# Fourier mixing and a routed expert layer on one core: the order of the second batch's loads and of its first stage at the start of the kernel

## The chip, the cores and the metric

The kernel runs on one core of one Trainium2 chip. The metric is the device time of the program in microseconds (us), median of the runs shown. One more execution was taken with the hardware profiler; every duration below that is not a median comes from that one.

## The reference, cut to what matters

```python
X = np.fft.fft(x, axis=1)              # x: (8, 2496, 256), over the sequence of 2496
x = np.fft.fft(X, axis=2).real         # over the 256 features; then (19968, 256) tokens
logits = x @ w_gate                    # 8 experts
e = argmax(logits); g = softmax(logits)[e]
h = np.maximum(x @ w1[e], 0.0)         # w1[e]: 256 x 1024
out = g * (h @ w2[e])                  # w2[e]: 1024 x 256, rows in the order of the tokens
```

Each of the eight batches is transformed, every token is sent to the one expert with the largest logit, and the expert's two matrix products follow. All data are 32-bit floats.

## The kernel before, in words

**Two parts.** The Fourier part works batch by batch. The sequence length is split as 2496 = 104 x 24. The first stage does the transforms of length 104, the second stage those of length 24, and in the same second stage a matmul (tile p, `p3` in the code) does the 256 features and the gate logits. The expert part works block by block: 128, 256 or 512 rows of one expert, fetched from a table of sorted rows in DRAM, `Xs`. A list made ahead of time (`rounds`, `in_order`) says which blocks may be computed once the rows of which batches are in `Xs`. The blocks of batch 0 alone are two of 256 and four of 128 rows.

**Loads of x.** A batch's x comes in three pieces of 896 KB (q = 0, 1, 2; tile xq, three buffers), each asked for by `load(b, q)` (L285, issue at L294) on the queue of SyncE (SP). Batch 0's third piece is asked for in two halves (L301).

**First stage.** `first(b)` (L387 to L410) is a generator of twelve steps, three for each of four rounds. Rounds 0 to 2 fold piece q on VectorE (`fold`, L320, and `fold_d`, L309 to L311: add and subtract mirrored rows and columns). Rounds 1 to 3 multiply the piece before on TensorE (`half1`, tile s, twice two columns), copy the result on ScalarE (L335, tile t) and write it to a DRAM tensor `Td` (L405; for batch 1 on ScalarE's queue); then `load` asks for the piece of the next batch into the freed buffer. In the text below the steps are counted 1 to 12: step 1 is the first fold of piece 0, steps 4 and 7 the first folds of pieces 1 and 2, steps 5, 8, 11 the first half of the products of pieces 0, 1, 2, and steps 6, 9, 12 the second half with the write to `Td`. Piece 2's second half is longer than the others: ten matmul instructions instead of four. After step 12, `ahead_of` (L991) asks with `regroup` (L414, issue at L417) for two DMAs that read `Td` back in the order that the second stage needs (tile t4s).

**Batch 0's first stage** is `first_whole` (L339). It doesn't go through DRAM: each of its twelve columns is sent by one SBUF-to-SBUF DMA of 110 KB from tile t (t1 in the code, two buffers) to every twelfth partition of t4s (L371), even columns on ScalarE's queue, odd ones on SP's. Loads of batch 1 stand between them on SP's queue: piece 0 ahead of column 9, pieces 1 and 2 behind column 11 (L373 and L374).

**Second stage.** `second(b)` (L425) is a generator of 19 steps, k = 0 to 18. Step 0 reads t4s (tile pr, L435), steps 1 and 2 transform the first two groups, each of steps 3 to 7 and 11 to 15 transforms one group more (tile p2 into zz, L443), multiplies for the features (tile p3) and makes the rows on VectorE (L474, twice); steps 8 to 10 and 16 to 18 are the routing of a half (`route`, L480 to L522: arg max, softmax, position in the expert's list). p3, p2, s and pr share three PSUM buffers. `send` (L526) sends 128 rows to their places in `Xs` with one indirect DMA of GpSimd (L237); a batch has 20 of them.

**The order of the work** is written out by the driver (L1054 to L1093): every engine executes its instructions in the order in which these generators are advanced. Before the change `early = ahead_of(1)`, batch 1's first stage, is advanced three steps ahead of `second(0)`, and then once after each even step k from 4 on, eight times in all. What is left of it, step 12 and the regrouping, comes later in `side`, woven with the making of the block table (`close`, `plan`, L542 on), while `experts` waits for its first table, for the sends and for twelve more steps of `side`.

**At the start** (L1015 to L1038) POOL asks for a table of constants, for `rt` and `wg` (from which a small product, tile pg, makes part of the table), for the constants of the plan (`bt`) and writes a block of padding rows to `Xs`. TensorE multiplies ones, WARM = 60 times, while x is on its way.

Of the kernel before, what the change touches and what calls it, by code (L numbers as in the profile page):

```python
# [12 lines left out]
F32 = mybir.dt.float32  # L13
# [7 lines left out]
B, S, D = 8, 2496, 256  # L21
# [3 lines left out]
NQ = NS // 4  # L25
# [4 lines left out]
NP = 112  # L30
# [6 lines left out]
E, F = 8, 1024  # L37
FC = F // 128
BIG, BLK, REST = 512, 256, 128
CAP = NT + BLK  # L40
# [11 lines left out]
def bc(ap, axis, n):  # L52
    shape = list(ap.shape)
    shape.insert(axis, n)
    return ap[tuple([slice(None)] * axis + [None])].to_broadcast(shape)
# [75 lines left out]
def rounds():  # L131

    want = [((256, 2), (128, 4)), ((256, 4),)] + [((512, B),)] * (B - 2)
    plan, used = [], 0

    def full(done, size):
        return max(0, -(-(done - used - E * (size - 1)) // size))

    for b in range(B):
        done = (b + 1) * S
        now = []
        for size, most in want[b]:
            k = min(full(done, size), most)
            if k:
                now.append((size, k, False))
            used += size * k
        if b == B - 1:
            k = full(done, BLK)  # L150
            used += BLK * k
            now.append((BLK, k, False))
            now.append((REST, (NT - used + E * (REST - 1)) // REST, True))
        plan.append(now)
    return plan
# [29 lines left out]
LATE = 4  # L185
SHARE, EARLY, ROOM = 0.6, 0.7, 1.2
AHEAD = 12
WARM = 60
MOST = max(k for now in rounds() for _, k, _ in now)


def halved(b, size):

    return size == 512 and b > 2 or size == 256 and b == B - 1
# [7 lines left out]
def block_consts():  # L202
    c = {
        "i": np.arange(MOST),
        "e9": np.arange(E + 1),
        "low": (np.arange(E)[None, :] <= np.arange(E)[:, None]).reshape(-1),
        "cap": CAP * np.arange(E),
    }
    at, k = {}, 0
    for n, v in c.items():  # L210
        at[n] = (k, k + len(v))
        k += len(v)
    return np.concatenate(list(c.values())).astype(np.float32)[None], at
# [3 lines left out]
def kernel(ctx: ExitStack, tc, x, w_gate, w1, w2, out):  # L217
    nc = tc.nc
    vec, act, pool = nc.vector, nc.scalar, nc.gpsimd

    def mm(o, lhsT, rhs, start=True, stop=True, **kw):
        nc.tensor.matmul(o, lhsT=lhsT, rhs=rhs, start=start, stop=stop, **kw)  # L222

    Td = [nc.dram_tensor(f"Td{b}", (NP, NS * D), F32, kind="Internal").ap() for b in range(B)]
    Xs = nc.dram_tensor("Xs", (ROWS, W), F32, kind="Internal").ap()

    def const_dram(name, v):
        return nc.inline_tensor(v, name=f"c_{name}").ap()

    def unordered(ins, group):  # L230
        ins = getattr(ins, "ins", ins)
        tc.declare_no_dep(ins, group=group, reason="no row is written twice")
        tc.add_to_no_dep_group(group, ins)
        return ins
# [7 lines left out]
    def sent(ins, b):  # L242
        tc.declare_no_dep(ins, group="taken", reason="no block before this batch's round has these rows")
        tc.add_to_no_dep_group(f"xs{b}", ins)
# [9 lines left out]
    xp = ctx.enter_context(tc.tile_pool(name="xp", bufs=2))  # L254
# [5 lines left out]
    pad = cp.tile([128, W], F32, name="pad")  # L260
# [9 lines left out]
    con, k = {}, 0  # L270
# [9 lines left out]
    wg = cp.tile([128, 2, E], F32, name="wg")  # L280
# [6 lines left out]
    def load(b, q, parts=1):  # L287

        if b < B:
            xq = xp.tile([NP, 8, D], F32, tag="xq", name="xq", bufs=3)  # L290
            row = (b * NQ + q) * NA
            ahead[b, q] = xq[0:NA]
            if parts == 1:
                nc.sync.dma_start(out=xq[:].rearrange("p j d -> p (j d)"), in_=x[row:row + NP])  # L294
                return iter(())
            return pieces(xq, row)

    def pieces(xq, row):

            for k in range(2):  # L300
                nc.sync.dma_start(  # L301
                    out=xq[:].rearrange("p (c j) d -> p c j d", c=2)[:, :, 2 * k:2 * k + 2],
                    in_=x[row:row + NP].rearrange("p (c j d) -> p c j d", c=2, d=D)[:, :, 2 * k:2 * k + 2])
                yield

    def fold_d(o, a, n):

        lo, hi = free(a, 1, [D, n], [1, H - 1]), free(a, D - 1, [D, n], [-1, H - 1])
        vec.tensor_tensor(free(o, 1, [D, n], [1, H - 1]), lo, hi, op=ALU.add)  # L309
        vec.tensor_tensor(free(o, H + 1, [D, n], [1, H - 1]), lo, hi, op=ALU.subtract)  # L310
        vec.tensor_copy(free(o, 0, [D, n], [H, 2]), free(a, 0, [D, n], [H, 2]))  # L311
# [27 lines left out]
    def first_whole():  # L339

        pm0 = xp.tile([NA, D], F32, tag="pm0", name="pm0")
        for q in range(NQ):
            xq = ahead.pop((0, q))
            t1 = xp.tile([NP, 4, D], F32, tag="t1", name="t1")
            for lo in (0, 2):
                end = q == NQ - 1 and lo
                a, m = xq[:, lo:lo + 2], xq[:, 4 + lo:6 + lo]
                n = 2
                if end:
                    n = 1  # L350
                    fold_d(pm0[:], m[:, 1], 1)
                vec.tensor_tensor(a[:, 0:n], a[:, 0:n], m[:, 0:n], op=ALU.add)
                fold_d(m, a, 2)
                ps = pm_.tile([NP, 2, D], F32, tag="m", name="s1")
                for i in range(2):
                    s = 4 * q + lo + i
                    o = ps[0:NR, i]
                    if s < NS - 1:
                        mm(o, columns(s), m[:, i])
                        continue  # L360
                    for k, l, r in ((NS - 1, 0, H + 1), (NS + 1, H + 1, D)):
                        mm(o[:, l:r], columns(k), pm0[:, l:r], True, False)
                        mm(o[:, l:r], columns(k + 1), m[:, 1, l:r], False, True)
                if end:
                    for i in range(2):
                        act.copy(t1[0:NR, lo + i], ps[0:NR, i])
                else:
                    act.copy(t1[0:NR, lo:lo + 2], ps[0:NR])
                for i in range(2):
                    s = 4 * q + lo + i  # L370
                    (nc.sync if s % 2 else act).dma_start(out=t4s[s:GP:NS, 0:NG], in_=t1[0:NR, lo + i])  # L371
            if q:
                load(1, q - 1)  # L373
        load(1, NQ - 1)  # L374
        for lo in range(0, NS + 3, 5):
            natural(lo, lo + 5)
        for h in range(2):
            ahead[0, "t4", h] = t4s[:, h * HALF:(h + 1) * HALF]

    def columns(s):  # L380
        return wp[:, s]

    def natural(lo, hi):
        n = hi - lo
        vec.tensor_copy(free(con["w1"][:, lo:hi], 0, [NP, n], [2 * NU, NG], [1, 2 * NU]),
                 free(wp[:, lo:hi], 0, [NR, n], [1, NG], [NG, 2 * NU]))
# [36 lines left out]
    zz = cp.tile([128, 2, NW * 128], F32, name="zz")  # L423
# [102 lines left out]
    def send():  # L526

        if waiting:
            b, place, idx, rows = waiting.popleft()
            if b:  # L530
                due = sp.tile([128, 1], F32, tag="due", name="due", bufs=8)
                act.copy(due[:], place)  # L532
                pool.tensor_copy(idx, due[:])  # L533
            sent(put_row(Xs, idx, rows, E * CAP - 1, "xs"), b)


    cv, where = block_consts()
    bt = cp.tile([1, cv.shape[1]], F32, name="bt")
# [463 lines left out]
    def mixed(b):  # L1002
# [22 lines left out]
    came = cp.tile([1, 1], F32, name="came")  # L1025
    pool.tensor_copy(came[:], wp[0:1, NS + 2, 0:1])
    pool.dma_start(out=table[:], in_=const_dram("table", packed))
    pool.dma_start(out=con["rt"][:], in_=const_dram("rt", consts["rt"]))
    pool.dma_start(out=wg[:], in_=w_gate)
    pool.dma_start(out=bt[:], in_=const_dram("blocks", cv))  # L1030
    sent(unordered(pool.dma_start(
        out=Xs[E * CAP:].rearrange("(k p) w -> p k w", k=BLK // 128), in_=bc(pad[:], 1, BLK // 128)), "xs"), 0)
    for k in range(WARM):
        pw = pse.tile([128, D], F32, tag="bd"[k % 2], name="py")
        mm(pw[:], ones[:], bc(ones[:], 1, 2))
# [4 lines left out]
    tabs, whole = {}, set()  # L1040
    todo = in_order()
    first_whole()
    vec.tensor_copy(tri[:], con["tri"][:])
    for c in range(2):
# [10 lines left out]
    for _ in range(3):  # L1055
        next(early)
    for k, _ in enumerate(second(0)):
        if k > 3 and k % 2 == 0:
            next(early, None)
        send()  # L1060
    work = experts(todo)
    steps = {b: mixed(b) for b in range(1, B)}
    for b in range(1, B):
# [6 lines left out]
        blocks = [(size, k * size / BIG, halved(b - 1, size)) for size, k, _ in rounds()[b - 1]]  # L1070
        total = sum(k * (15 if seven_ else 16) for _, k, seven_ in blocks)
        open_ = sum(k * (8 if seven_ else 16) for _, k, seven_ in blocks)
        while done < total:
            w, full = next(work)
# [72 lines left out]
```

## Time and profile before

| | |
|---|---|
| median of 3 runs | 1264.88 us (1259.51 to 1265.91) |
| profiled execution | 1264.07 us, span of its trace 1262.3 us |
| TensorE busy | 1213.0 us, 96% of the span |
| VectorE, ScalarE, GpSimd busy | 763.6, 430.8, 449.2 us |
| mean granted TensorE clock | 0.979 |
| TensorE busy in 0 to 110 us, and from there to 1262 us | 73.4 of 110 us; 1139.7 of 1152 us |

The trace counts from the start of the span; 1.8 us of the profiled execution lie outside of it. PE is TensorE's matmul, PEld its weight load, DVE VectorE, ACT ScalarE, POOL GpSimd, SP SyncE; a q behind the name of an engine is its sequencer, which issues DMAs. In a line of the timeline the first number is the start in us, the second the duration, then engine, line of the code, operation, output and input tile, and in brackets how long the engine stood idle before and what it waited for. In a line of the chain of waits stand start, duration, and the work that the end of the program was waiting for at that time.

### The profile page before, as it was taken

What the parts mean: (1) busy time and instruction counts of PE and PEld (TensorE: products, weight loads), DVE (VectorE), ACT (ScalarE), POOL (GpSimd) and SP (SyncE); (2) the same over time, 40 slices, a digit from 0 to 9 for tenths busy, and PEclk for the clock granted to TensorE, in tenths of its full rate; (3) what the DMA queues carried; (4) which work ended last, traced back from release to release, by engine and by line L of the source; (5) the groups of instructions that cost most, each with busy time, mean ns of one, the idle gap of its engine ahead of it and who ended that gap; (6) DMA issues with size and microseconds to landing.
All of it is one profiled execution on the core that took longest, in us unless ns stands there. A gap on an engine that the chain in (4) does not pass through costs nothing.

```text
span 1262.3 us, 22419 instructions
## 1 busy us (share of the span) xinstructions
PE 1213.0 (96%) x7333; PEld 1080.0 (86%) x7333; DVE 763.6 (60%) x1820; ACT 430.8 (34%) x1168; POOL 449.2 (36%) x533
## 2 busy tenths in 40 slices
PE   6759999999999999999999999999999999999997
PEld 3648898777788899888988899889999999999996
DVE  4564424343455688566866578686888884444663
ACT  1423332332243433434343333432332232222222
POOL 1234527154117512472226613472364241111112
PEclk8779999999999999999999999999999999999999
DMA  9579999773648434673346435443346238788877
GB/s 227 139 255 330 300 330 319 200 236 132 154 153 260 155 114 163 180 236 116 101 127 208 137 103 169 139 162 101 117 136 196 92 109 299 276 284 289 271 272 281
DMA packets 162899, 248.31 MB, mean 197 GB/s; under 512 B 118572, under 2 KB 129974, under 8 KB 143311
## 3 DMA queue, kind: packets, MB, share of 16 engines
q1 hardware_dynamic: 145370, 201.53, 50.8%
q0 software_dynamic: 16192, 43.11, 9.7%
q10 hardware_dynamic: 1221, 2.24, 0.6%
q8 instruction: 59, 0.97, 0.3%
q14 instruction: 57, 0.47, 0.1%
HBM read 193.45 MB, written 53.45 MB: 196 GB/s over the span
## 4 chain that ended last, share of the span: by engine, by line
PE 85%; DVE 8%; DMA 3%; ACT 2%; issue 2%; SPq 0%; ACTq 0%; POOL 0%; POOLq 0%; DVEq 0%
PE py L222 25%; PE ph L222 13%; PE a L222 11%; PE c L222 10%; PE p L222 7%; PE b L222 6%; PE d L222 5%; PE e L222 4%; PE s L222 4%; DMA t4s<-t 1%; DVE xT L648 1%; DVE y L748 1%; DMA xb<-Xs 1%; DVE hT L700 0%; DVE hT L706 0%
## 5 line engine op out<-in xcount | busy, mean ns | idle before, releaser
L237 POOL DMA_INDIRECT out_dram<-y,ro x163 | 161.1, 988 | 628.1 <-ACT y L744 291.1
L222 PE MATMUL py<-w_sb,hT 128*128 128x256 f32 x1504 | 339.7, 379 | 0.0
L222 PEld LDWEIGHTS py<-w_sb,hT 128*128 128x128 f32 x1504 | 281.4, 190 | 36.9 <-issue 1.0
L237 POOL DMA_INDIRECT Xs<-rows,pi x160 | 162.0, 1013 | 89.5 <-POOL pi L533 41.7
L222 PE MATMUL ph<-xT,w_sb 128*128 128x128 f32 (+2 forms) x992 | 171.8, 329 | 4.5 <-DVE ro L857 4.5
L222 PEld LDWEIGHTS ph<-xT,w_sb 128*128 128x128 f32 x992 | 137.3, 193 | 28.9 <-issue 16.8
L474 DVE SCALAR_TENSOR_TENSOR rows<-p,zs 128x129 f32<-128x129 f32 x160 | 48.8, 348 | 136.7 <-ACT lg L472 136.2
L222 PE MATMUL a<-xT,w_sb 128*128 128x256 f32 (+1 forms) x512 | 118.1, 358 | 1.1 <-DVE xT L648 1.1
L902 DVE TENSOR_SCALAR hT<-ph 128x512 f32<-128x512 f32 x43 | 29.7, 691 | 131.7 <-PE ph L222 71.8
L222 PEld LDWEIGHTS a<-xT,w_sb 128*128 128x128 f32 x512 | 88.4, 190 | 11.8 <-DVE xT L648 2.3
L651 ACT ACTIVATE xT<-xT 128x256 f32<-128x256 f32 (+1 forms) x94 | 36.5, 388 | 175.8 <-DVE xT L648 132.0
L956 ACT ACTIVATE y<-py,xb 128x256 f32<-128x256 f32 x94 | 44.4, 473 | 150.7 <-PE py L222 149.0
L700 DVE TENSOR_TENSOR hT<-hT,b 128x512 f32<-128x512 f32 x57 | 39.2, 688 | 74.7 <-PE b L222 48.9
L710 ACT ACTIVATE hT<-a 128x512 f32<-128x512 f32 x57 | 34.0, 597 | 134.3 <-PE a L222 129.8
L533 POOL CAST pi<-due 128x1 int32<-128x1 f32 x140 | 44.2, 316 | 73.7 <-ACT due L532 73.6
L222 PE MATMUL a<-w_sb,hT 128*128 128x128 f32 x528 | 66.0, 276 | 0.0
L222 PEld LDWEIGHTS a<-w_sb,hT 128*128 128x128 f32 x528 | 63.1, 192 | 0.7
L222 PEld LDWEIGHTS p<-table,t4s 120*128 120x128 f32 x352 | 54.7, 205 | 9.0 <-issue 2.6
L222 PE MATMUL c<-xT,ws 128*128 128x256 f32 (+1 forms) x256 | 60.3, 362 | 0.8
L222 PE MATMUL p<-table,t4s 120*128 120x120 f32 (+1 forms) x352 | 57.7, 290 | 1.9 <-ACT t4s L436 1.9
L222 PE MATMUL p<-table,zz 128*128 128x145 f32 (+1 forms) x320 | 57.3, 303 | 2.2 <-ACT zz L443 1.3
L222 PE MATMUL b<-xs,ws 128*128 128x256 f32 (+1 forms) x256 | 58.7, 356 | 0.0
(164 smaller groups left out, 2071.2 us busy)
## 6 DMA issues: line engine op xcount, KB each, us to landing
w_sb<-in_moe_w_dram SPq DMA_DIRECT2D x132, 1024.0 KB
xq<-in_x_dram SPq DMA_DIRECT2D x23, 896.0 KB
xb<-Xs SPq DMA_DIRECT2D x112, 128.0 KB
Td<-t SPq DMA_DIRECT2D x18, 448.0 KB
t4s<-Td SPq DMA_DIRECT2D x7, 768.0 KB
t4s<-Td SPq DMA_DIRECT2D x7, 640.0 KB
xb<-Xs SPq DMA_DIRECT2D x52, 64.0 KB
xb<-Xs SPq DMA_DIRECT2D x88, 32.0 KB
```

What stands on the lines that cost most here:

```text
L222: nc.tensor.matmul(o, lhsT=lhsT, rhs=rhs, start=start, stop=stop, **kw)
L237: return unordered(pool.indirect_dma_start(out=dst, out_offset=bass.IndirectOffsetOnAxis(ap=idx, axis=0), in_=rows, in_offset=None, bounds ...
L474: vec.scalar_tensor_tensor(rows[:, k + m, 0:NY], p3[:, 0:NY], zs[:, 0:1], zs[:, 1:], op0=ALU.add, op1=op)
L533: pool.tensor_copy(idx, due[:])
L648: vec.transpose(free(xT[:], 256 * h, [32, n // 32], [BIG, 2], [1, 32]), free(xb, 512 * h, [64, n // 32], [1, 2], [2, 32]))
L651: act.activation(odd, odd, ACTF.Copy, scale=-1.0)
L700: vec.tensor_tensor(h12, h11, b[:], op=add)
L710: act.activation(h11, a[:], ACTF.Relu)
L748: vec.tensor_tensor(o, o, p[:], op=add)
L902: vec.tensor_scalar(o, ph[:], 0.0, None, op0=ALU.max)
L956: act.activation(y[:, i % 2], py[:], ACTF.Copy, scale=meta[:, i, 1:2])
```

## The change

Six edits.

- Batch 1's three loads of x are asked for after all twelve SBUF-to-SBUF DMAs of batch 0, no longer between them. Behind them on SP's queue now follow the DMA of `bt` and that of the padding rows, which POOL issued before.
- The last third of `first_whole` writes its results not to a third t1 tile, which is the buffer of the first third, but into a part of zz that is not yet in use.
- POOL asks for `wg` ahead of `rt`.
- WARM is 44 instead of 60.
- `early` is advanced after the steps k of `second(0)` that PLAN names, as often as it says, ten times in all, instead of after each even k from 4 on. So step 4 of `first(1)` follows k = 3, step 5 k = 5, step 6 k = 7, step 7 k = 11, step 8 k = 12, steps 9 and 10 k = 13, step 11 k = 14, step 12 k = 15.
- With that, the regrouping of batch 1 (two DMAs, then the load of batch 2's piece 2) is issued after k = 16, ahead of the last steps of batch 0's routing and not in `side`.

```diff
-WARM = 60
+WARM = 44
+PLAN = {3: 1, 5: 1, 7: 1, 11: 1, 12: 1, 13: 2, 14: 1, 15: 1, 16: 1}
...
             xq = ahead.pop((0, q))
-            t1 = xp.tile([NP, 4, D], F32, tag="t1", name="t1")
+            if q < NQ - 1:
+                t1 = xp.tile([NP, 4, D], F32, tag="t1", name="t1")
+            else:
+                t1 = zz[0:NP, 0, 0:4 * D].rearrange("p (j d) -> p j d", d=D)
...
                     (nc.sync if s % 2 else act).dma_start(out=t4s[s:GP:NS, 0:NG], in_=t1[0:NR, lo + i])
-            if q:
-                load(1, q - 1)
-        load(1, NQ - 1)
+        for q in range(NQ):
+            load(1, q)
+        nc.sync.dma_start(out=bt[:], in_=const_dram("blocks", cv))
+        sent(unordered(nc.sync.dma_start(
+            out=Xs[E * CAP:].rearrange("(k p) w -> p k w", k=BLK // 128), in_=bc(pad[:], 1, BLK // 128)), "xs"), 0)
...
     pool.dma_start(out=table[:], in_=const_dram("table", packed))
+    pool.dma_start(out=wg[:], in_=w_gate)
     pool.dma_start(out=con["rt"][:], in_=const_dram("rt", consts["rt"]))
-    pool.dma_start(out=wg[:], in_=w_gate)
-    pool.dma_start(out=bt[:], in_=const_dram("blocks", cv))
-    sent(unordered(pool.dma_start(
-        out=Xs[E * CAP:].rearrange("(k p) w -> p k w", k=BLK // 128), in_=bc(pad[:], 1, BLK // 128)), "xs"), 0)
...
     for k, _ in enumerate(second(0)):
-        if k > 3 and k % 2 == 0:
+        for _ in range(PLAN.get(k, 0)):
             next(early, None)
         send()
```

## The prediction

> **What bounds the kernel now.** I read the slices of the page first, then TensorE's waits late and early, then the chain of waits and the timeline of the first 110 us.
>
> ```profile
> PE   6759999999999999999999999999999999999997
> PEclk8779999999999999999999999999999999999999
> DMA  9579999773648434673346435443346238788877
> ```
>
> From the fourth slice (31.6 us each) on PE is full; the DMA engines are busy but not what PE waits for. The losses lie in slices one to three, where the clock is low as well. By stretches (us of the stretch, then busy PE, PEld, DVE, ACT, POOL, clock, DMA share, GB/s):
>
> ```profile
> 12.40:24.00 11.60, 7.43 (x37) 5.63 (x35) 7.80 (x25) 3.57 (x7) 3.26 (x6) 0.86 0.90 247
> 24.00:34.00 10.00, 0.94 (x4) 0.84 (x4) 2.90 (x6) 0.00 (x0) 0.00 (x0) 0.50 0.97 222
> 60.00:75.00 15.00, 4.41 (x25) 3.49 (x25) 13.77 (x63) 1.75 (x4) 11.95 (x11) 0.67 0.77 265
> 90.00:110.00 20.00, 15.88 (x84) 13.73 (x85) 8.51 (x32) 6.93 (x25) 3.50 (x6) 0.83 0.91 303
> ```
>
> Three holes: 9 us before 34, 10 us in 60 to 75, 4 us before 94. The waits name two of them (this list covers 36 to 110 us, in the earlier list the line is "PE pr L222 <- DMA t4s<-t: 9.2"):
>
> ```profile
> PE pr L222 <- DMA t4s<-Td: 10.1, 1, 10.1
> PE rk L222 <- DVE oh L495: 5.4, 2, 3.3
> PE ph L222 <- DVE ro L857: 4.5, 1, 4.5
> ```
>
> Both big ones are t4s: first batch 0's twelve DMAs, then batch 1's regrouping. The chain shows the same path:
>
> ```profile
> 1.35 11.27 PE py L222 x60
> ...
> 17.20 7.89 DMA t4s<-t
> ...
> 25.15 8.41 DMA t4s<-t
> ...
> 66.48 3.08 DMA Td<-t
> ...
> 69.68 6.08 DMA t4s<-Td
> ```
>
> Column 11 is issued at 25.15 and lands at 33.56; its issue waited for the landing of the DMA sent at 17.20, column 4, which in the order of SP's and ACT's DMAs is eight issues earlier. It takes 8.41 us for 110 KB, since batch 1's x shares the engines. Batch 0's second stage starts at 34.13:
>
> ```profile
> 29.89 1.22 DVE L320 TENSOR_TENSOR xq<-xq 104x1024 f32<-104x1024 f32 x1 [4.61 <-DMA xq<-in_x_dram]
> 34.13 0.54 PE L222 MATMUL pr<-t4s,table 120*120 120x6 f32 x2 [9.19 <-DMA t4s<-t]
> ```
>
> **What the Trainium skill says.** "DMA: Bandwidth & Descriptors", section "Issuing engines are not separate DMA queues": all queues run on the same 16 DMA engines. The trace agrees: at a share of 0.97 in 24 to 34 us, 110 KB took 8.41 us. The same page, "Why a DMA increments its semaphore by 16 and not by 1": SP's and ACT's DMAs use the largest number up to 16 that divides the slowest dimension of both sides; for 110 source rows and 10 target partitions that is 10 engines. No row here shows it; I use it for the late bound of the landing. "TensorE: Matmul & The Clock Gate", Part 1: the clock falls to half after an idle window of about 3.4 us and comes back after a busy one. Agrees: 0.50 in 24 to 34 us, and 1.0 again at 38, 3.8 us after PE started.
>
> **The change, part by part.** Times are of the trace; the sum is made against the profiled 1264.07.
>
> *WARM 44.* 60 took 11.27, so 16 fewer free PE 3.0 earlier (9.6 for 12.6; the first fold ends at 9.66). But the last half of batch 0's x arrives at 16.94 (VectorE waits for it until then) and the last products, which end at 20.56, hang on that. Gain on the path 0. Cost: columns sent earlier take 1 to 1.4 from that x (three of 113 thousand bytes at 250 GB/s), or the clock halves ahead of the last 1.53 us of products. Between 0 and +1.5; I take +0.5.
>
> *zz as third buffer.* ScalarE's copy at 21.68 waited 3.06 for the first third's DMAs; it can go at 19.5. The last two copies (0.65) then follow the products: 20.6 + 0.5 + 0.7 = 21.8 for the last issue, where it was 25.15. The first write of zz (L443) has to wait for these DMAs, but its input is what they bring: 0.
>
> *x behind the twelve.* Windows to 17 us moved 3.66 MB, of which 3.44 were batch 0's load, so some 0.2 of the twelve. Left: 12 x 0.113 + table 0.44 + rt 0.26 - 0.2 = 1.85 MB. At 247 GB/s that is 7.5 us, so 24.5; if only ten engines take the 1.15 MB of columns left and ten sixteenths of the rest (1.6 MB at 10/16 of 247), 10.4, so 27.4. Landing adds 1 to 2 (a POOL row DMA into idle engines took 2.4). Bounds 25.5 to 29; taken 27.0. pr starts at 27.1: **-7.0**.
>
> *What comes late next.* VectorE is in order, and batch 1's first folds stand ahead of batch 0's first L474. x(1,0) was issued at 19.58 and landed at 29.89; now it is issued at 22.5 at the earliest (eight issues earlier is again column 4, now sent near 16 with less beside it; if that still took 7.9 us, 24), and follows the columns: 25.5 + 0.92 MB / 247 + 1.3 = 30.5 (29 to 33). The folds took 2.6 (29.89 to 32.52), so the first L474 goes at 33.1, not at 27.1 + 4.5 = 31.6. x(1,1) is 3.7 later, 34.2, and its fold now follows k = 3: the second L474 at 35.4 (was 39.90). The third was behind that fold before, so it comes at about 36.1 for 41.56. Left of the 7.0: **-5.2** (3 to 7). bt and padding are behind x on SP; the padding is needed late and bt at 63.6: 0. wg ahead of rt: pg needs both, lands about 23: 0, as pr comes later.
>
> *PLAN.* Steps 11 and 12 come ahead of the second routing. Step 11 (four matmuls 1.0, copy 0.6) delays the last rows by some 1.2 (0 to 3). Step 12 is behind the last p3 on PE, so its ten matmuls delay no row; its copy and DMA issue (0.6 + 0.3) stand ahead of L500 on ACT while VectorE does 1.4 of arg max: 0. Routing ends at 63.5 - 5.2 + 1.2 = 59.5. POOL sends 20 times from 51.57 to 79.01 without a gap over 0.31; from 46.4 on the ten of the second half are due at 59.5, just when they are ready: last send 73.8, -5.2.
>
> *Regrouping.* The last p3 ended at 58.1, now 54.1. Step 12 takes 2.6 (2.0 at full clock, 3.2 at half), the copy 0.6: Td at 57.3 for 66.48. Landing 3.1, regroup 6.1, issue 0.2 as before: pr of batch 1 at 66.8 for 75.90, **-9.1** (-6 to -11). Behind the regrouping's wait on SP stand the load of batch 2's piece 2 and the first weights, as before (72.40): no new waiter.
>
> *First block.* From that pr to the first ph it took 18.0 (75.90 to 93.89), VectorE busy to the end; `side` is one step further there, +0.5: 85.3. The other path, rows: last send 73.8, landing 2.5 to 6.2, five issues 2.5, landing at most 5.4: 82 to 88. I take 85.3, **-8.6**.
>
> *To the end.* In 110 to 1262 PE is idle 12.5 us, its waits there sum to 4.6: all of it moves up. DMA is 0.91 to 0.96 busy to 200 us, so +0.5 (0 to 2).
>
> Sum: -8.6 + 0.5 = -8.1; 1264.07 - 8.1 = **1256.0**. The profiled execution lies 0.8 under the median 1264.88, inside their scatter; I add nothing.
>
> **Rivals.**
> *More.* The columns land at 25.5, x(1,0) at 29, step 11 hides: -7 at the first routing, -11 at regrouping and block: 1253, with a fuller clock 1251. For it: full DMA rate (377 GB/s at 20 to 21 us). Against: nearly full engines. 0.12.
> *The wait moves.* x lands at 33 or the sends become last (88): the saving at the first block is 3 to 5. 1260.5. For it: VectorE's order, and the same bytes before 38 us, DMA being nearly full until then. 0.20.
> *Slower: the clock.* 44 ones end early, PE then works in pieces with gaps, as rows wait for x. If it stays at 0.5 from 14 us to the first block, some 18 us of matmuls that ran at full clock between 34 and 94 take 36: +18 less what fits into holes, 12 to 18, against -8: 1268 to 1276, taken 1272. It decides from about 8 us of such matmuls. Against: a long busy piece restored the clock each time. 0.10.
> The forecast has 0.58.
>
> **The numbers.** About 0.5% (6.3 us, below 1258.6 or above 1271.2) is what a measurement can tell from no change. Faster: 0.12 + 0.58 x 0.87 and a bit of the second rival, 0.63. Slower 0.08, from the clock. Same 0.29. The range 1250 to 1264 leaves out the clock's 0.10 and the ends of the others.
>
> **What would show it.** pr of batch 0 near 27 (34.13), first L474 near 33, behind an L320 that waits for x; last send near 74; pr of batch 1 near 67; first ph near 85; PE full after 110 us. It is wrong if the columns still land at 30, if L474 waits for x beyond 36, if the first block waits for rows, or if the clock row shows 5 or 6.

## The result, and the profile after

The changed kernel takes 1256.67 us (median of 9 runs, 1252.7 to 1260.38), the kernel before in the same sets of runs 1262.69 (9 runs, 1259.51 to 1265.91). The ratio is 0.9949 with a 95% interval of 0.9933 to 0.9965, so 4.4 to 8.5 us less; the medians lie 6.0 us apart. The forecast was 1256.0. The profiled execution went from 1264.07 to 1256.62 us (span 1262.3 to 1254.8). Of the experiments below, the first four ran beside the kernel before at 1262.63 us and the later sets beside it at 1286.71, 1289.58 and 1287.80 us, so each ratio is to the kernel before in its own set, single times of a trace are compared within a set, and one execution of 7136.73 us (of the kernel with the rows first) is left out.

In the table, pr is the first product of a second stage, ph the first product of the expert part (x @ w1), with which the first block starts, and x(1,0) further below is piece 0 of batch 1's x.

| | before | forecast | after |
|---|---|---|---|
| pr of batch 0 starts | 34.13 | 27.1 | 25.57 |
| batch 1's piece 0 of x is folded from | 29.89 | 30.5 | 30.23 |
| rows of batch 0: first, second, third L474 | 38.65, 39.90, 41.56 | 33.1, 35.4, 36.1 | 32.77, 35.41, 36.56 |
| last of the 20 sends ends | 79.01 | 73.8 | 74.03 |
| batch 1's last write to Td: issue, landing | 66.48, 3.08 | 57.3, 3.1 | 55.50, 5.55 |
| pr of batch 1 starts | 75.90 | 66.8 | 67.22 |
| first ph | 93.88 | 85.3 | 85.57 |

Lines of the code have moved: L474 before is L480 after, L320 is L321, L417 is L423. The slices of the page, each now 31.4 us:

```profile
PE   7569999999999999999999999999999999999997
PEclk8779999999999999999999999999999999999998
DMA  8679899873649443763347435443446238788887
```

TensorE is still not full before the fourth slice. By stretches (columns as in the prediction: us of the stretch, busy PE, PEld, DVE, ACT, POOL, then clock, DMA share, GB/s) the hole before 34 us has gone, the second one is still there, in part ahead of 60 us now:

```profile
24.00:34.00 10.00, 7.23 (x38) 6.79 (x38) 3.48 (x10) 2.81 (x11) 0.00 (x0) 0.74 1.00 250
60.00:75.00 15.00, 7.79 (x33) 7.14 (x34) 9.17 (x42) 3.06 (x10) 11.28 (x10) 0.55 0.88 297
90.00:110.00 20.00, 19.71 (x117) 17.20 (x117) 9.14 (x37) 8.89 (x36) 8.55 (x15) 0.98 1.02 370
```

TensorE's waits from 0 to 110 us say the same. The wait for batch 0's columns (9.2 us) is no longer in the list; the wait for the regrouping is about as long as before (10.8 against 10.1), only earlier; the wait for ro, the row numbers of the first block, is also as before (4.7 against 4.5); new are waits for VectorE's folds (tile xq) and for its rows:

```profile
PE pr L223 <- DMA t4s<-Td: 10.8, 1, 10.8
PE ph L223 <- DVE ro L863: 4.7, 1, 4.7
PE s L223 <- DVE xq L312: 3.6, 5, 1.9
PE p L223 <- DVE rows L480: 3.0, 2, 2.2
```

The timeline shows what has taken the columns' place. pr waits only for the part of the table that comes from the small product pg (0.42 us), and then VectorE stands in front of x:

```profile
25.57 0.54 PE L223 MATMUL pr<-t4s,table 120*120 120x6 f32 x2 [0.42 <-DVE table L1054]
...
30.23 1.23 DVE L321 TENSOR_TENSOR xq<-xq 104x1024 f32<-104x1024 f32 x1 [4.74 <-DMA xq<-in_x_dram]
...
32.77 0.60 DVE L480 SCALAR_TENSOR_TENSOR rows<-p,zs 128x129 f32<-128x129 f32 x2
...
34.27 1.23 DVE L321 TENSOR_TENSOR xq<-xq 104x1024 f32<-104x1024 f32 x1 [0.90 <-DMA xq<-in_x_dram]
35.41 0.60 DVE L480 SCALAR_TENSOR_TENSOR rows<-p,zs 128x129 f32<-128x129 f32 x2
```

The first rows had their inputs at 30 us (their copy on ScalarE ended at 29.99) and waited for the folds of x(1,0); the second ones waited for the fold of x(1,1). In the chain of waits up to 130 us a load of x therefore stands where the columns stood. It is that of x(1,1), which lands at 34.24 and whose fold stands ahead of the second rows. Behind it comes a landing of Td that is longer than before:

```profile
23.22 11.02 DMA xq<-in_x_dram
...
55.50 5.55 DMA Td<-t
61.18 5.90 DMA t4s<-Td
```

### The profile page after: what moved, and what is told of

Read it like the earlier page. It is cut to its first block, busy times and chain, and to the rows that moved or that the text cites. A ratio compares the mean times of both kernels' runs of the same rounds, so it can differ in the third digit from the quotient of the medians.

```text
span 1254.8 us, 22389 instructions
## 1 busy us (share of the span) xinstructions
PE 1210.5 (96%) x7317; PEld 1077.9 (86%) x7317; DVE 761.5 (61%) x1820; ACT 431.8 (34%) x1168; POOL 448.0 (36%) x531
## 4 chain that ended last, share of the span: by engine, by line
PE 65%; issue 17%; DVE 8%; DMA 4%; POOL 3%; ACT 2%; SPq 0%; POOLq 0%; DVEq 0%; ACTq 0%
PE py L223 19%; PE a L223 9%; PE c L223 8%; PE ph L223 7%; PE p L223 6%; PE b L223 5%; PE d L223 4%; PE e L223 3%; PE s L223 3%; POOL out_dram L238 3%; DMA xq<-in_x_dram 2%; DVE xT L654 1%; DMA Td<-t 1%; DMA t4s<-Td 1%; DVE y L754 1%
## 5 line engine op out<-in xcount | busy, mean ns | idle before, releaser
L480 DVE SCALAR_TENSOR_TENSOR rows<-p,zs 128x129 f32<-128x129 f32 x160 | 48.8, 347 | 128.2 <-ACT lg L478 122.1
```

What stands on the lines that cost most here:

```text
L480: vec.scalar_tensor_tensor(rows[:, k + m, 0:NY], p3[:, 0:NY], zs[:, 0:1], zs[:, 1:], op0=ALU.add, op1=op)
```

## The experiments

**Theory.** Nearly all of the gain comes from the order of the loads: the twelve columns no longer share the DMA engines with batch 1's x. From then on VectorE's folds, which wait for x, hold the rows up, so that the ones, the zz buffer and part of the columns' gain are worth nothing more. PLAN brings Td forward, but little of it reaches the end. **Rivals:** the ones and the buffer are part of the gain; PLAN is the gain; the rows of batch 0 decide and PLAN is worth nothing.

**One edit each on the kernel before.** The loads alone:

```diff
-            if q:
-                load(1, q - 1)
-        load(1, NQ - 1)
+        for q in range(NQ):
+            load(1, q)
```

> The kernel before with one edit: batch 1's three loads behind all twelve columns (60 ones, third t1 tile, old interleaving, bt and padding on POOL stay). Theory (the columns no longer share the DMA engines with batch 1's x; after that VectorE's folds, which wait for x(1,0), set the pace): the third third still waits for the buffer of the first, so the last column goes out near 24 and lands near 27; pr of batch 0 near 27.5 (34.13 before), first L474 near 34 (38.65), because x(1,0) now lands near 31; pr of batch 1 near 72 (75.90), first ph near 90 (93.89); 3 to 4 us faster than before, half of the whole change. Rival (the gain is the ones and the zz buffer): columns still land at 30 or later, 0 to 1 us. Rival (x late eats all): L474 stays at 38 or later, 0.

Measured: 1257.47 us, ratio 0.9959 (0.9946 to 0.9972): 5.2 us of the whole change's 6 by the medians (the two intervals overlap). One of the last columns now takes 3.84 us, where it took 8.41. pr of batch 0 starts at 27.76, and the first rows run right behind the folds:

```profile
22.62 3.84 DMA t4s<-t
...
30.74 1.23 DVE L320 TENSOR_TENSOR xq<-xq 104x1024 f32<-104x1024 f32 x1 [4.55 <-DMA xq<-in_x_dram]
...
33.28 0.60 DVE L473 SCALAR_TENSOR_TENSOR rows<-p,zs 128x129 f32<-128x129 f32 x2
34.43 0.61 DVE L473 SCALAR_TENSOR_TENSOR rows<-p,zs 128x129 f32<-128x129 f32 x2 [0.54 <-ACT lg L471]
```

pr of batch 1 starts at 70.12 and the first ph at 86.84, better than the 72 and 90 expected. With the old interleaving the second rows don't even wait for x(1,1). The columns are as expected, the share is larger. What comes behind them is nearly a tie in this trace: the first rows' inputs are ready at 32.41, so the folds hold them by 0.9 us only, and the chain of waits runs over TensorE's products, whose clock was 0.50 from 20 to 32 us.

PLAN alone:

```diff
+PLAN = {3: 1, 5: 1, 7: 1, 11: 1, 12: 1, 13: 2, 14: 1, 15: 1, 16: 1}
...
-        if k > 3 and k % 2 == 0:
+        for _ in range(PLAN.get(k, 0)):
```

> The kernel before with PLAN alone (and the regrouping after k = 16). Theory: start unchanged (pr of batch 0 at 34.1); step 12 ahead of the second routing brings batch 1's Td from 66.5 to about 62.5 and its pr from 75.9 to about 72 to 73; the rows of batch 0 go out no earlier (last send 79 to 80), so the first block gets 1 to 3 us earlier, 91 to 93; 1 to 3 us faster than before. Rival (the plan is what matters): 5 us or more. Rival (the denser plan delays the rows, and they decide): 0 or slower.

Measured: 1261.38 us, ratio 0.9989 (0.9979 to 0.9998): some 1.4 us. Td's last write leaves at 62.40, 4.1 us earlier, as expected. But it lands in 5.99, where the loads-only kernel has 3.08. The chain of the PLAN-only kernel:

```profile
62.40 5.99 DMA Td<-t
68.51 6.25 DMA t4s<-Td
```

and of the loads-only kernel:

```profile
60.83 3.08 DMA Td<-t
64.04 5.94 DMA t4s<-Td
```

So 1.0 us is left at pr (74.90) and 1.1 at the first ph (92.82). The product of the two ratios, 0.9948, agrees with the 0.9949 of the whole change. It leaves nothing that could be told for wg ahead of rt and for the move of bt and the padding rows, which have no kernel of their own.

**One edit each taken back from the change.** 60 ones:

```diff
-WARM = 44
+WARM = 60
```

> The changed kernel with 60 ones again. Theory: the ones are off the path, since the last half of batch 0's x (16.7) gates the last products and the DMA of rt gates pr: pr of batch 0 within 0.5 us of 25.6, time within 1 us of the changed kernel (6 us faster than before). The clock may stay at full rate for the last products (they took 2.4 us at half clock in the changed kernel, 1.5 before). Rival (fewer ones are part of the gain): 2 to 3 us slower than the changed kernel.

Measured: 1258.43 us, ratio 0.9959 (0.9947 to 0.9971), no difference from 0.9949 that the intervals could tell. pr of batch 0 starts at 27.80, 2.2 later than in the changed kernel: that part of the expectation was wrong. But the first L480 is at 33.12 against 32.77, since x(1,0) is folded from 30.58. Most of what pr gains VectorE doesn't use. The last products take 2.34 us with 60 ones too, so the clock falls ahead of their end with either number.

The third t1 tile in the place of zz:

```diff
-            if q < NQ - 1:
-                t1 = xp.tile([NP, 4, D], F32, tag="t1", name="t1")
-            else:
-                t1 = zz[0:NP, 0, 0:4 * D].rearrange("p (j d) -> p j d", d=D)
+            t1 = xp.tile([NP, 4, D], F32, tag="t1", name="t1")
```

> The changed kernel with a third t1 tile in the place of zz, so the last third's copies wait for the first third's columns again. Theory: with x gone from between, these land by 18 to 20, before the last products (21.0) need the buffer's second half; first copy 16.8 to 18 or later, last column issued at 21.5 to 22.5; pr at 25.6 to 26.5; time within 1 us of the changed kernel. Rival (the buffer was a wait of its own, 3.06 us in the kernel before): columns 2 to 3 us later, first L474 up to 1 us later, 1 to 2 us slower than the changed kernel.

Measured: 1255.96 us, ratio 0.9945 (0.9929 to 0.9961), the same. The wait for the buffer is back, and hidden: this copy waits 3.31 us and ends at 19.93, ahead of the last products, whose copies follow at 21.22:

```profile
19.34 0.59 ACT L369 COPY t<-s 110x512 f32<-110x512 f32 x1 [3.31 <-DMA t4s<-t]
```

pr starts at 25.94, the first rows at 32.26.

These two traces also show how far a single trace can be trusted. Their medians don't differ from the change's beyond the intervals, and yet Td leaves at 53.48 and 52.89 in them (55.50 in the change's trace) and the first ph starts at 82.94 and 82.75 (85.57). The granted clock differs. The same stretch in the change, with 60 ones, and with the third t1 tile:

```profile
34.00:60.00 26.00, 18.14 (x108) 14.78 (x106) 18.12 (x71) 11.72 (x41) 10.31 (x11) 0.80 0.64 190
...
34.00:60.00 26.00, 15.85 (x112) 12.82 (x111) 20.01 (x76) 12.27 (x44) 12.03 (x12) 0.95 0.64 199
...
34.00:60.00 26.00, 15.00 (x106) 12.06 (x104) 19.98 (x81) 11.37 (x40) 12.63 (x12) 0.94 0.64 195
```

So up to 2.8 us between two traces at the first ph need not come from an edit, and the 1.0 and 1.1 us that PLAN alone shows are below that.

The old interleaving:

```diff
-        for _ in range(PLAN.get(k, 0)):
+        if k > 3 and k % 2 == 0:
```

> The changed kernel with the old interleaving (a step after every even k from 4 on, the rest with the regrouping woven in later). Theory: pr of batch 0 stays at 25.6 and the first L474 at 32.8; steps 11 and 12 come behind the second routing again, so batch 1's Td leaves at 60 to 61 in place of 55.5 and its pr starts at 69.5 to 70.5 (67.2); first ph 87.5 to 88.5 (85.6): 2 to 3 us slower than the changed kernel, 3.5 to 5 faster than before. Rival (the plan brings nothing, as the rows decide): the same as the changed kernel. Rival (the plan is most of the gain): 5 us or more slower.

Measured: ratio 0.9959 (0.9939 to 0.9979), against 0.9946 (0.9924 to 0.9968) of the change in a later set: the same 0.1% that PLAN alone brought, not resolved here. Td's last write, pr of batch 1 and the first ph come at 63.83, 73.06 and 90.43, all later than expected; no trace of the change itself was taken in this set.

**The longer landing of Td.** In the changed kernel step 9 asks for batch 2's piece 1 at 50.34, 5 us ahead of Td's last write; piece 0 was asked for at 42.63. Both moved behind the regrouping:

```diff
-                if b > 1 or b and q < NQ:
+                if b > 1:
                     load(b + 1, q - 1)
...
         if b == 1:
-            load(b + 1, NQ - 1)
+            for q in range(NQ):
+                load(b + 1, q)
```

> The changed kernel with batch 2's loads 0 and 1 asked for behind the regrouping of batch 1, where load 2 is. In the changed kernel batch 1's last write to Td took 5.55 us to land beside those two loads (3.08 before the change). Theory: it lands in 3, pr of batch 1 near 64.7 (67.2); batch 2's first fold (59.5) then waits for x near 67 to 68 and holds the plan of the blocks up, so the first weights leave near 69 to 71 (64.3); first ph 83 to 85.5: 0 to 2.5 us faster than the changed kernel. Rival (VectorE's order again: the fold that waits for x delays rows and tables by more than is won): the same or up to 3 us slower.

Measured: ratio 0.9994 (0.9967 to 1.0021): no gain is left that could be told. Td, issued at 60.25, lands in 3.07, as expected. But batch 2's first fold waits for x until 74.62 (10.34 us), the first weights leave only at 79.36 and the first ph starts at 94.60. The rival was right about VectorE's order.

Only piece 1 moved, so that the first fold has its data:

```diff
-                if b > 1 or b and q < NQ:
+                if b > 1 or b and q == 1:
                     load(b + 1, q - 1)
...
-            load(b + 1, NQ - 1)
+            for q in range(1, NQ):
+                load(b + 1, q)
```

> The changed kernel with only batch 2's piece 1 asked for behind the regrouping; piece 0 stays where it was, so that VectorE's first fold of batch 2 has its data. Theory: batch 1's last Td lands in 3 to 4 us (5.55 in the changed kernel), pr of batch 1 1.5 to 2.5 us earlier, the fold of piece 1 waits until 66 to 67 in a hole of VectorE; first ph 1 to 2.5 us earlier; 0.5 to 2 us faster than the change. Rival (as with both loads moved: folds that wait hold the tables and the weights up): the same or slower.

Measured: ratio 0.9969 (0.9951 to 0.9987), not better than the change's 0.9946. The second fold waits now, in front of the tables of the next blocks, and the first ph starts at 91.83 (85.81 in the change of the same set):

```profile
74.71 1.23 DVE L321 TENSOR_TENSOR xq<-xq 104x1024 f32<-104x1024 f32 x1 [6.49 <-DMA xq<-in_x_dram]
```

These two kernels show what it costs when a fold waits for x. They are no test of what a shorter landing brings: in the change's own trace of the second of these sets Td's last write landed in 3.07 us as well, with both loads in place. It left late there (58.31), since ScalarE stood still for 5.1 us ahead of the copy before it, though TensorE had written the input by 52.85; nothing in the trace says why. Over all traces, those of the kernels further below too, the landing goes with the time from the load of batch 2's piece 1 to this write:

| kernels | load asked for ahead of the write, us | landing of the write, us |
|---|---|---|
| the change, PLAN alone, 60 ones, third t1 tile | 5.16 in each | 5.55, 5.99, 5.35, 5.77 |
| rows first, the first time | 7.60 | at most 4.0 |
| before, loads alone | 8.87, 8.71 | 3.08, 3.08 |
| the change in the later set, eleven steps, eleven steps with rows first | 9.97, 11.34, 9.88 | 3.07, 3.07, 3.06 |
| rows first again, old interleaving | 9.95, 11.15 | at most 3.2 and 3.3 |
| both loads behind, piece 1 behind | asked for later | 3.07, 3.07 |

So the landing is long where a transfer is near, and PLAN makes it near. That this is the cause is likely; no edit shows it alone. Step 9's own write to Td (448 KB), 0.6 us behind that load, comes nearer with it, and which of the two counts is not separated.

**VectorE's order.** Steps 1 to 3 behind k = 3, so that the first rows go ahead of the folds:

```diff
-PLAN = {3: 1, 5: 1, 7: 1, 11: 1, 12: 1, 13: 2, 14: 1, 15: 1, 16: 1}
+PLAN = {3: 3, 4: 1, 6: 1, 7: 1, 11: 1, 12: 1, 13: 2, 14: 1, 15: 1, 16: 1}
...
     early = ahead_of(1)
-    for _ in range(3):
-        next(early)
```

> The changed kernel with steps 1 to 3 of batch 1's first stage (both folds of piece 0) behind k = 3 and step 4 behind k = 4, step 5 behind k = 6. Theory: in the changed kernel the first L474 (32.8) waited only because VectorE had to fold x(1,0) first, which landed at 30.2; now it runs at 30.1 and the second at about 33, the third at 35.5 behind the fold of x(1,1); the routing of the first half starts 0.5 to 2 us earlier; 0 to 1.5 us faster than the changed kernel. Rival (x(1,1) sets the pace anyway): no difference.

Measured: ratio 0.9932 (0.9908 to 0.9956). The first L480 runs at 31.11, a microsecond later than expected, but directly behind its input.

> The change itself once more, as the measure for its three neighbours on the same chip. Every theory: ratio to the kernel before 0.993 to 0.9965, as at first.

Measured: ratio 0.9946 (0.9924 to 0.9968).

> The changed kernel with steps 1 to 3 of batch 1's first stage behind k = 3 (step 4 behind k = 4, step 5 behind k = 6), measured beside the change itself, since the first time every kernel of its round was slow by 24 us. Theory (VectorE's order makes the first rows wait for x(1,0)): first L474 1.5 us earlier, as the first time, and 0 to 2 us faster than the change. Rival (x(1,1) sets the pace anyway): within 0.5 us of the change.

Measured: ratio 0.9933 (0.9911 to 0.9955). The first rows need no longer wait for x, which the timeline shows directly (their wait ends with ScalarE's copy lg):

```profile
29.69 0.61 DVE L480 SCALAR_TENSOR_TENSOR rows<-p,zs 128x129 f32<-128x129 f32 x2 [4.48 <-ACT lg L478]
30.22 1.22 DVE L321 TENSOR_TENSOR xq<-xq 104x1024 f32<-104x1024 f32 x1
...
32.74 0.60 DVE L480 SCALAR_TENSOR_TENSOR rows<-p,zs 128x129 f32<-128x129 f32 x2
33.27 1.22 DVE L321 TENSOR_TENSOR xq<-xq 104x1024 f32<-104x1024 f32 x1
```

In the change's first trace the first rows stood 2.8 us behind their inputs, so that the folds held them up is shown. Against the change of the same set the first three rows are 3.3, 2.3 and 1.8 us earlier, Td 1.1 and the first ph 0.7. Of that the edit has only a part: pr starts 2.5 us earlier in this trace (25.26 against 27.74), and in the change's the first rows' inputs were ready only at 32.42, 0.55 us before they ran. What the edit is worth at the end (0.9932 and 0.9933 against 0.9946) is under the intervals.

**The step that PLAN takes from `side`.** Between 94 and 200 us TensorE idles 0.5 us before the change, 1.0 with the loads alone, and 2.2 with PLAN, alone or in the change. One step of `side` less ahead of the first block:

```diff
-                for _ in range(12):
+                for _ in range(11):
                     yield 0, False
```

> The changed kernel with eleven steps of side work, not twelve, before the first block is turned, so that batch 1's second stage is as far then as in the kernel before. Theory (PLAN uses up step 12 early, and side is one step further at the first block and after it; the waits that this brings cost 1.2 to 1.7 us between 94 and 200 us and 0.5 ahead of the first ph): first ph 0.3 to 0.8 us earlier, PE idle in 94 to 200 us about 1 us as in the loads-only kernel (2.2 in the changed one), 1 to 2 us faster than the change. Rival (those waits come from the DMA engines, which are nearly full there): no difference.

Measured: ratio 0.9898 (0.9862 to 0.9934), six runs. The first ph starts at 90.11 in this trace, 4.3 us later than in the change of the same set and not earlier as expected; Td's last write, which leaves ahead of the edit, is already 4.7 us later, so this tells nothing of it. From 94 to 200 us TensorE idles 4.1 us, 4.7 in the change and 6.3 in the kernel with the rows first, of the same set.

> Both small edits on top of the change: steps 1 to 3 of batch 1's first stage behind k = 3, and eleven steps of side work ahead of the first block. Theory (the first saves 1.5 us at the first rows, the second the waits between 94 and 200 us): first L474 near 30 to 31, ratio to the kernel before 0.989 to 0.993, that is under the change's 0.9946 to 0.9949. Rival (eleven steps bring nothing; their 0.9898 came from six runs of a disturbed round): 0.993 to 0.9955.

Measured: ratio 0.9921 (0.9893 to 0.9948), seven runs; first L480 at 29.77, first ph at 83.83 (85.08 in the kernel with the rows first alone, of another set). TensorE's waits behind the start of the first block, up to 200 us, in the change of the later set (hT is the result of ph after the maximum with 0):

```profile
PE p L223 <- ACT t4s L442: 2.3, 1, 2.3
PE py L223 <- DVE hT L908: 1.6, 2, 1.3
```

and with eleven steps, alone in the same set or with the rows first:

```profile
PE py L223 <- issue: 2.2, 1, 2.2
PE p L223 <- ACT t4s L442: 0.9, 1, 0.9
```

The wait for hT is gone, and in its place stand 2.2 us for nothing that the trace shows. With both edits TensorE idles 3.4 us from 94 to 200 us. By the ratios, eleven steps alone have 0.9898 against the change's 0.9948 +- 0.0013 (both its measurements, weighted by their intervals), from six runs; but on top of the rows first they have 0.9921 against the 0.9932 and 0.9933 of the rows first alone, which is no difference. So what eleven steps are worth is open, and so is the way by which it would come.

## Why the prediction was right

The mechanism held, and most times along the path; sizes differ, in both directions. That the time came within 1 us of the forecast is in part luck: the sum started from a profiled execution 1.4 us above the median of the nine runs, and it took off 8.1 us where the medians have 6.0.

- **WARM and zz: 0 on the path.** Right at the end, by the two kernels that take them back. With 60 ones pr starts 2.2 us later, so at pr it was not 0; the folds hide most of it. The bound was right that the clock could fall during the last products (10 matmuls from 18.55 to 20.98, 2.4 us for 1.53), but fewer ones are not the reason, since it fell with 60 ones as well, and it cost nothing that shows. Nor need the window ahead be idle, as the prediction has it: in the trace before the change the clock fell at 20.9 us, with TensorE busy 1.5 of the 3.4 us ahead of that. The step "zz as third buffer" counted the saved wait into an earlier last issue; with columns that go out early this wait is hidden without zz too.
- **x behind the twelve: -7.0, was -8.6 at pr.** The columns had landed by 25.57, ahead of the taken 27.0 and near the early bound; pr waited for pg, which the sum had put at nothing because pr would come later. The late bound, ten DMA engines at the mean rate, was too late. It made no difference, because of the next step.
- **What comes late next: -5.2 left.** The strongest step. x(1,0) came at 30.2 (30.5 forecast), the rows at 32.77, 35.41, 36.56 (33.1, 35.4, 36.1). Loads alone show that the order of the loads is the gain: 5.2 us at the end.
- **PLAN and regrouping: -9.1, was -8.7 at pr of batch 1.** Two terms were off and cancelled, which is luck. Td left 1.8 earlier than forecast, and its landing, taken over as 3.1, was 5.55. The step said of the moved work only what waits behind it; it forgot the transfers that the neighbouring step 9 starts, which are now close ahead of Td. Where these come 5.16 us ahead of it, it took 5.35 to 5.99 us, and 3.08 in the kernel before and with the loads alone, where they come 8.7 us or more ahead. So PLAN alone leaves 1 us at pr of the 4 by which it moves Td.
- **First block: -8.6, was -8.3.** By way of VectorE, as forecast; the rows were in time.
- **To the end: +0.5 taken, 1.7 measured** between 94 and 200 us. The reason given, full DMA engines, is not the main one: the loads alone lose 0.5 there with the engines as full (share 0.97, 0.95 in the change). PLAN takes the rest: TensorE idles 2.0 to 2.2 us there with PLAN alone, in the change, with 60 ones and with the third t1 tile, 0.5 in the kernel before. Whether that is `side` being one step further, which the sum had priced only at the first block, the kernels with eleven steps don't settle.
- **Rivals.** "The wait moves" was right in kind, x is the next wait, but x(1,0) was there at 30.2 and not at 33, and the first block came 8.3 us earlier and not 3 to 5. "Slower: the clock" happened in small: the clock came back to full at 29 us, fell to half again from 36 to 43, and the two traces where it stayed full in this stretch have the first ph 2.6 and 2.8 us earlier. The 12 to 18 us of that rival did not come. Two slips of the working changed nothing: its own 12 to 18 less 8 end at 1274 and not 1276, and TensorE idles 12.35 us in 110 to 1262, with waits of 4.5, where it says 12.5 and 4.6.

## What to carry to other kernels

When a late transfer is the wait, list what its consumer needs besides, with the time at which each comes: here pr came 8.6 us earlier and the first rows 5.9, because they now stand behind batch 1's x, and two further edits that brought pr forward bought nothing that could be told. A step that is moved takes its transfers with it, so look at what the DMA engines carry in the few microseconds ahead of each landing that the path waits for. And before a load is put behind the landing that it disturbs, look for an engine with a fixed order that holds an instruction which needs the load: here the first ph came 6.0 us later that way. A difference of 1 or 2 us between two single traces is not yet the edit's; compare the clock of the stretch first.

## What the runs showed of the hardware

Transfers of 110 KB from SBUF to SBUF took 7.89 and 8.41 us while loads of x were in the queues with them (the kernel before), and 3.84 and 4.48 us with these loads behind them (loads alone, and 60 ones). A write of 448 KB to DRAM landed in 3.06 to 3.08 us (at most 3.3 in two more traces) where a load of 896 KB had been asked for 8.7 us or more ahead of it, and in 5.35 to 5.99 us where it had been asked for 5.16 us ahead. And one program had its first block 2.6 to 2.8 us later than two with nearly the same times at the end, in traces that differ in the clock between 34 and 60 us: 0.80 against 0.95 and 0.94.
